# Two kernels in one: halves of k and v moved from the lower and upper partitions to the even and odd ones

## The chip, the cores and the metric

The kernel runs on one core of a Trainium2 chip. The metric is device time of one execution in microseconds: the median of three runs of the kernel before is 225.6 us, and they lie between 224.6 and 225.98. A profile of one further execution shows what each engine did. The engines are TensorE (PE; its weight loads are listed as PEld), VectorE (DVE), ScalarE (ACT), GpSimd (POOL) and SyncE (SP), which here only issues transfers.

## The reference

Two independent computations on 2048 tokens of 576 channels are placed side by side in the output.

```python
# A: attention of 32 heads (18 channels each) over 8 earlier tokens, two apart
q, k, v = split(x @ wqkv)
idx = pos[:, None] - 2 * arange(8)                 # masked where negative
a = softmax(einsum(q, k[idx]) * 18 ** -0.5) @ v[idx]
a = a.reshape(S, D) @ wo
# B: a short and a long causal convolution per channel, gated
k_shift = sum(k_pad[t : t + S] * shift_k[:, 3 - t] for t in range(4))
kv = k_shift * v
y = causal_convolution(kv, ssm_k) + kv * ssm_D     # length 2048, by FFT in the reference
b = q * y
out = concatenate([a, b], axis=-1)
```

## The kernel before

**Part A.** x is brought into transposed form (channels in partitions) in two ways. Its first two quarters of 512 tokens are loaded as they are (`load_x`, line 150) and turned on TensorE (`transpose_x`, `tail_x`, lines 403 to 412), then copied from PSUM by VectorE and ScalarE (lines 464 to 467 for the first quarter, 474 to 476 for the second). The second half comes by a transposing transfer (`turn_x`, line 207). Projections follow: `project_first` (line 433) for the first two quarters of q, then units of `project` (line 307). The logits are products on VectorE (line 647), summed over the channels of a head on TensorE (line 656); softmax runs on VectorE and ScalarE; the weights are spread over partitions by transfers on SP (line 724), multiplied with v on VectorE (line 746) and summed on TensorE (line 762); `output` (line 799) multiplies with wo.

**Part B.** The long convolution is done in four blocks of 512 tokens by matrix products with tables of sines. Each block is stored in two halves of 64 partitions. In the lower half, partition p holds seven consecutive rows of k, of which the last four are tokens 4p to 4p+3 of the block; the three before them serve the short convolution. The upper half holds the block's last 256 tokens mirrored, that is in descending order. `load_k` (line 157) and `load_v` (line 174) issue one transfer for each half; for the first block the low half is split, since rows before the first token don't exist: three rows of zeros (line 164), the first four tokens (line 165), and the rest in two pieces (line 168). `taps` (line 502) forms the short convolution on VectorE: four products and three sums per block, and a product with v (lines 507 to 511). Its coefficients `skb` must run forwards in one half and backwards in the other. The loop at line 445 makes them: a row of the coefficients is copied to all partitions by matmuls with a matrix of ones, `ones96`, one matmul for the lower 64 partitions and one for the upper 64. `mirror` (line 513) multiplies each block with the matrix `fold` (lines 228 to 231), which puts the sum of a token and its mirror image in one half and their difference in the other. The spectra of the filter (`filter_spectrum`, line 543, ps_fk) and of the blocks (`x_spectrum`, line 602, ps_fx), their products (line 883), sums (ps_z, line 903) and the inverse (ps_inv and ps_back, lines 935 to 976) follow; VectorE multiplies with q (line 989) and the result is stored.

**The order of the work.** The order of every engine is written out by the program. VectorE runs through tables, taps, logits, softmax, weighted sums and spectral products. TensorE's other work lies in a list of units, and at each step of VectorE's sequence the function `until` (line 283) issues as many units as the next number in the tuple `PLACES` (line 19) says. `need` issues units until those of a given name are done. SP's queue holds, in this order: x's first quarter in two transfers, the first third of the weights (`load_w(nc.sync, 0)`), x's second quarter, k's first block, the second third of the weights, `turn_x(0)`, v's first block, k's second block, `turn_x(1)`, v's second block, and later the rest. A transfer that reuses a semaphore waits for the one that used it before; there are eight. Before the first x arrives, `idle_work` (line 137) keeps TensorE busy with matmuls of zeros, four at the start and two after the coefficients.

**PSUM.** Two tags, A and B, of two buffers each, serve all results of TensorE; the coefficients use B, A and A in the three passes of the loop at line 445.

Of the kernel before, what the change touches and what calls it, by code (L numbers as in the profile page):

```python
# [12 lines left out]
ALU = mybir.AluOpType  # L13
FP32 = mybir.dt.float32
BF16 = mybir.dt.bfloat16
# [1 line left out]
PSUM = bass.MemoryType.PSUM  # L17

PLACES = (
    16, 6, 8, 11, 1, 0, 5, 2, 0, 4, 2, 4, 1, 0, 4, 2, 3, 0, 1, 2, 1, 3, 2, 4, 0, 1, 6, 3, 2, 6, 3, 5, 0, 7, 5,  # L20
    2, 4, 0, 0, 1, 2, 1, 0, 3, 0, 1, 0, 0, 0, 0, 5, 1, 0, 4, 0, 0, 3, 0, 0, 0, 3, 0, 4, 4, 1, 1,
)


def view(t, offset, dims):

    return bass.AP(tensor=t.tensor, offset=t.offset + offset, ap=[list(t.ap[0])] + [list(d) for d in dims])
# [3 lines left out]
def kernel(  # L31
# [13 lines left out]
    nc = tc.nc  # L45
    Bsz, S, D = A_x.shape
# [3 lines left out]
    xf = A_x.flatten_outer_dims()  # L50
    outf = out.flatten_outer_dims()
    qf = B_q.flatten_outer_dims()
    kf = B_k.flatten_outer_dims()
    vf = B_v.flatten_outer_dims()
# [14 lines left out]
    NBL, BL = 4, 512  # L69
# [18 lines left out]
    def bank2(name, tag):  # L88
        return pp.tile([128, 2, 512], FP32, name=name, tag=tag)
# [12 lines left out]
    def xT(kb, t0, n):  # L102
        return view(xw, XW + SPB * (t0 // 1024) + 1024 * kb + t0 % 1024, [[1, n]])

    def x5(jj):
        return view(xw, XW + SPB * jj + 4096, [[1, 512]])
# [14 lines left out]
    sp1 = s1.enter_context(tc.tile_pool(name="s1", bufs=1, reuse_waits="tile"))  # L121
# [6 lines left out]
    nc.scalar.dma_start(skrow[96:97, :], B_shift_k.rearrange("d j -> (d j)").unsqueeze(0))  # L128
    warm = sp1.tile([128, 1], FP32, name="warm")
    nc.scalar.activation(warm[:], pib[:], ACT.Sin)  # L130
    ones96 = sp1.tile([97, 64], BF16, name="ones96")
    nc.vector.memset(ones96[0:96, :], 0.0)
    nc.vector.memset(ones96[96:97, :], 1.0)
    nc.vector.memset(skrow[0:96, :], 0.0)
    ones0 = main.tile([128, 128], BF16, name="ones0")

    def idle_work(n):
        ps = bank2("ps_idle", "A")
        for _ in range(n):
            nc.tensor.matmul(ps[:, 0, :], zeros[:, 0:128], zeros, start=True, stop=True)  # L140
# [4 lines left out]
    xnat = view(Ks, 0, [[4 * D, 4], [D, 4], [1, D]])  # L145
# [1 line left out]
    kTok = main.tile([128, NBL, 4, D], BF16, name="kTok", tag="r_ktok")  # L147
    kjs, vts = [], []

    def load_x(qtr, sb0=0, n=4):  # L150
        r0 = 512 * qtr + 128 * sb0
        nc.sync.dma_start(xnat[:, qtr, sb0:sb0 + n], xf[r0:r0 + 128 * n, :].rearrange("(sb p) c -> p sb c", p=128))

    for sb in (0, 2):
        load_x(0, sb, 2)

    def load_k(i):

        eng = nc.sync
        kj = sp1.tile([128, 7, D], BF16, name="kj", bufs=2)  # L160
        r0 = BL * i
        low = [(0, 64)]
        if i == 0:
            nc.gpsimd.memset(kj[0:1, 0:3, :], 0.0)
            eng.dma_start(kj[0:1, 3:7, :], kf[0:4, :].unsqueeze(0))
            low = [(1, 49), (49, 64)]
        for p0, p1 in low:
            eng.dma_start(kj[p0:p1], bass.AP(tensor=kf.tensor, offset=kf.offset + (r0 + 4 * p0 - 3) * D,
                                             ap=[[4 * D, p1 - p0], [D, 7], [1, D]]))
        eng.dma_start(kj[64:128], bass.AP(tensor=kf.tensor, offset=kf.offset + (r0 + 256 + 3) * D,  # L170
                                          ap=[[4 * D, 64], [-D, 7], [1, D]]))
        kjs.append(kj)

    def load_v(i):
        vt = sp1.tile([128, 4, D], BF16, name="vt", bufs=2)
        nc.sync.dma_start(vt[0:64], vf[BL * i:BL * i + 256, :].rearrange("(p c) d -> p c d", c=4))
        nc.sync.dma_start(vt[64:128], bass.AP(tensor=vf.tensor, offset=vf.offset + (BL * i + 256 + 3) * D,
                                              ap=[[4 * D, 64], [-D, 4], [1, D]]))
        vts.append(vt)

# [13 lines left out]
    for gi, g in enumerate(GORD):  # L194
        sg = 1 - 2 * (g & 1)
        nc.gpsimd.iota(fr_i[:, gi, :], pattern=[[8 * sg, 128]], base=4096 * (g & 1) + sg * (2 * g + 1),
                       channel_multiplier=0)
    ones128 = sp1.tile([128, 128], BF16, name="ones128")
    nc.gpsimd.memset(ones128[:], 1.0)
    ident = main.tile([128, 128], BF16, name="ident")  # L200
    nc.gpsimd.affine_select(ident[:], ones128[:], pattern=[[1, 128]], compare_op=ALU.is_equal, fill=0.0,
                            base=0, channel_multiplier=-1)
# [4 lines left out]
    def turn_x(h):  # L207
# [15 lines left out]
    flip = main.tile([128, 128], BF16, name="flip")  # L223
    nc.gpsimd.affine_select(flip[:], ones128[:], pattern=[[1, 128]], compare_op=ALU.is_equal, fill=0.0,
                            base=-127, channel_multiplier=1)
    flipn = main.tile([128, 128], BF16, name="flipn")
    nc.gpsimd.tensor_scalar(flipn[:], flip[:], -1.0, None, op0=ALU.mult)
    fold = main.tile([128, 128], BF16, name="fold")
    for h in range(2):
        nc.gpsimd.tensor_copy(fold[0:64, 64 * h:64 * h + 64], ident[0:64, 0:64])  # L230
        nc.gpsimd.tensor_copy(fold[64:128, 64 * h:64 * h + 64], (flip, flipn)[h][64:128, 0:64])
    flip2 = main.tile([128, 128], BF16, name="flip2")
    nc.gpsimd.tensor_scalar(flip2[:], flip[:], 2.0, None, op0=ALU.mult)

# [1 line left out]
    for c0, p0, p1 in ((0, 0, 128), (128, 0, 128), (256, 0, 128), (384, 0, 128), (512, 0, 64), (512, 64, 128)):  # L236
        EHS.append(main.tile([128, 32], BF16, name=f"E{len(EHS)}"))
        e = EHS[-1][p0:p1, :]
        if p1 - p0 < 128:
            nc.gpsimd.memset(EHS[-1][64 - p0:128 - p0, :], 0.0)  # L240
        nc.gpsimd.affine_select(e, ones128[p0:p1, 0:32], pattern=[[-18, 32]], compare_op=ALU.is_ge, fill=0.0,
                                base=c0, channel_multiplier=1)
        nc.gpsimd.affine_select(e, e, pattern=[[18, 32]], compare_op=ALU.is_ge, fill=0.0,
                                base=17 - c0, channel_multiplier=-1)
# [3 lines left out]
                            fill=-1.0e9, base=-DIL * (W - 1), channel_multiplier=0)  # L248
# [125 lines left out]
    def table(n_i, T, vec, cols, period, offs):  # L374
        for n in range(2):
            nc.vector.tensor_scalar(n_i[:, n, :], vec, rp[:, cols[n]:cols[n] + 1], offs[n], op0=ALU.mult, op1=ALU.add)
        nc.vector.tensor_single_scalar(n_i, n_i, period - 1, ALU.bitwise_and)
        return lambda: nc.scalar.activation(T, n_i, ACT.Sin, bias=pib[:], scale=-2.0 * np.pi / period)

    def table_k(c):  # L380
        return table(n_all[:, 2 * c:2 * c + 2, :], TK[:, c, :, :], n_all[:, 8, :], (c, c), 2048, (512.0, 0.0))

    def table_x(n):
        n_i = view(qk, 4096 * n + 1024, [[2048, 2], [1, 1024]]).bitcast(I32)
        return table(n_i, TX[:, 2 * n:2 * n + 2, :], n_all[:, 8, :], (4 + 2 * n, 5 + 2 * n), 4096,
              (offx[:], offx[:]))
# [16 lines left out]
    def transpose_x(qtr, pts, kb0, sbs):  # L403
        for kb in (kb0, kb0 + 1):
            for sb in sbs:
                nc.tensor.transpose(pts[:, kb - kb0, 128 * sb:128 * sb + 128],
                                    xnat[:, qtr, sb, 128 * kb:128 * kb + 128], ident[:])

    def tail_x(qtr, pt):
        for sb in range(4):  # L410
            nc.tensor.transpose(pt[64 * qtr:64 * qtr + 64, 0, 512 + 128 * sb:640 + 128 * sb],
                                xnat[:, qtr, sb, 512:576], ident[:], tile_position=(0, 64 * qtr))

    def copy_tail(qtr, pt):
        r = slice(64 * qtr, 64 * qtr + 64)
        nc.scalar.activation(x5(0)[r], pt[r, 0, 512:1024], ACT.Copy)

    def pair_x():
        return pp.tile([128, 2, 1024], BF16, name="ps_x", tag="B")
# [13 lines left out]
    def project_first(jp, ct0):  # L433

        ps = bank2("ps_proj", "A")
        for e in range(2):
            c0 = 128 * (ct0 + e)
            for kb in range(4):
                nc.tensor.matmul(ps[:, e, :], wq(kb, 0, c0, 128), xT(kb, 512 * jp, 512), start=(kb == 0), stop=False)  # L439
        for e in range(2):  # L440
            nc.tensor.matmul(ps[:, e, :], wq(4, 0, 128 * (ct0 + e), 128)[64 * jp:64 * jp + 64],
                             x5(0)[64 * jp:64 * jp + 64], start=False, stop=True, tile_position=(64 * jp, 0))
        nc.scalar.activation(view(q, S * ct0 + 512 * jp, [[S, 2], [1, 512]]), ps[:], ACT.Copy)

    for n0 in (512, 0, 256):
        n = min(256, D - n0)
        ps = bank2("ps_sk", "A" if n == 256 else "B")
        for h in range(0, n, 128):
            w = min(128, n - h)
            sk = skrow[:, 4 * (n0 + h):4 * (n0 + h + w)].rearrange("p (d j) -> p d j", j=4)  # L450
            for r in range(2):
                nc.tensor.matmul(ps[64 * r:64 * r + 64, h // 128, 0:4 * w], ones96[:],
                                 sk if r else view(skrow, 4 * (n0 + h) + 3, [[4, w], [-1, 4]]),
                                 start=True, stop=True, tile_position=(0, 64 * r))
        nc.scalar.activation(skb[:, :, n0:n0 + n],
                             ps[:].rearrange("p b (d j) -> p j (b d)", j=4)[:, :, 0:n], ACT.Copy)
    sines = [table_k(0), table_k(1)]
    idle_work(2)
    pts = [pair_x() for _ in range(2)]
    for sbs in ((0, 1), (2, 3)):  # L460
        for n in range(2):
            transpose_x(0, pts[n], 2 * n, sbs)
    tail_x(0, pts[1])
    for n in range(2):
        nc.vector.tensor_copy(xT(n, 0, 512), pts[0][:, n, 0:512])
        nc.scalar.activation(xT(2 + n, 0, 512), pts[1][:, n, 0:512], ACT.Copy)
    copy_tail(0, pts[1])
    sines += [table_x(0), table_x(1), table_k(2), table_k(3)]
    project_first(0, 0)
    pts = [pair_x() for _ in range(2)]  # L470
# [98 lines left out]
    for i in range(NBL):  # L569
        r = taps(i)  # L570
# [450 lines left out]
    for n, (j, t, i) in enumerate(todo):  # L1021
# [3 lines left out]
        r = sums(j, t, i, *prs.pop(n))  # L1025
# [43 lines left out]
```

## Time and profile before

| | |
|---|---|
| median of three runs | 225.6 us (224.6 to 225.98) |
| the profiled execution | 225.71 us, of which span 224.0 |
| granted TensorE clock, mean | 0.987 of full speed |
| busy: TensorE, VectorE, ScalarE, GpSimd | 210.8, 208.0, 155.0, 34.3 us |
| transfers | 31.4 MB, 140 GB/s on average over the span |
| first product of the taps | 17.32 us after the span's start |
| first logits product | 62.87 us |

The span runs from the first to the last instruction that the profile has; the execution's own time holds a little more. Busy time is the time in which an engine works on at least one instruction. In a list in order of time, the first two numbers of a line are start and duration (for merged instructions the duration from the first to the last), the number behind the x is how many were merged, and the bracket says how long the engine was idle before and what it waited for. In the lists of waits the numbers are total microseconds, times, and the longest.

### The profile page before, as it was taken

How to read it: one execution, taken by the hardware profiler on the slowest of the kernel's cores; microseconds unless marked ns; L12 is line 12 of the kernel's file. 1: busy time of each engine (PE TensorE's matmuls, PEld its weight loads, DVE VectorE, ACT ScalarE, POOL GpSimd, SP SyncE). 2: the span in 40 equal slices, each digit the busy share in tenths (PEclk: the TensorE clock that was granted, in tenths of full speed). 3: DMA queues.
4: the chain of work that ended last, by engine and by line, in shares of the span. 5: the costliest groups of instructions: out<-in, count | busy, mean ns of one | idle time of the engine just before them, and what ended most of it. 6: DMA issues, size and time to landing. Idle time of an engine off the chain costs nothing.

```text
span 224.0 us, 5300 instructions
## 1 busy us (share of the span) xinstructions
PE 210.8 (94%) x2258; PEld 117.4 (52%) x2268; DVE 208.0 (93%) x154; ACT 155.0 (69%) x213; POOL 34.3 (15%) x71
## 2 busy tenths in 40 slices
PE   7869988999999999999999999999999999999892
PEld 2433343444575556663444446665656667667561
DVE  7958969999998999999989999999999899999992
ACT  5454799897676997655566758885678887655631
POOL 8981000000000040404320000005000000330000
PEclk9979999999999999999999999999999999999998
DMA  5999999999920038568999469907311103662016
GB/s 174 255 215 183 219 215 219 220 190 236 230 55 0 3 58 155 96 116 151 197 207 234 122 115 205 245 6 217 104 56 53 57 3 107 196 215 69 3 49 162
DMA packets 31001, 31.41 MB, mean 140 GB/s; under 512 B 16865, under 2 KB 26721, under 8 KB 30978
## 3 DMA queue, kind: packets, MB, share of 16 engines
q1 hardware_dynamic: 25728, 21.92, 45.5%
q0 software_dynamic: 2624, 6.64, 14.1%
q10 hardware_dynamic: 2626, 2.52, 3.3%
q8 instruction: 17, 0.28, 0.5%
q14 instruction: 6, 0.05, 0.1%
HBM read 13.11 MB, written 4.72 MB: 80 GB/s over the span
## 4 chain that ended last, share of the span: by engine, by line
PE 56%; DVE 15%; DMA 11%; ACT 7%; issue 4%; SPq 4%; DVEq 0%; ACTq 0%
PE ps_fk L538 9%; PE ps_wo L815 7%; PE ps_proj L311 6%; DVE qk L883 6%; PE ps_z L903 5%; DMA X<-attn 5%; PE ps_fk L539 5%; DMA Ks<-in_A_x_dram 4%; PE ps_inv L935 4%; PE ps_acc L762 3%; DVE P L746 3%; PE ps_log L656 3%; PE ps_proj L439 3%; SPq L724 3%; PE ps_fx L609 3%
## 5 line engine op out<-in xcount | busy, mean ns | idle before, releaser
L883 DVE TENSOR_TENSOR qk<-xw,Ks 128x3072 bf16<-128x3072 bf16 x30 | 50.5, 1753 | 1.2 <-PE ps_z L903 1.0
L647 DVE TENSOR_TENSOR prod<-qk 128x4096 bf16<-128x4096 bf16 (+1 forms) x20 | 40.6, 2075 | 2.7 <-PE ps_log L656 2.6
L311 PE MATMUL ps_proj<-xw 128*128 128x512 bf16 x151 | 36.9, 380 | 1.6 <-ACT qk L347 0.9
L538 PE MATMUL ps_fk<-kTok,TK 128*128 128x384 bf16 x128 | 32.8, 327 | 0.2 <-ACT Ks L553 0.2
L539 PE MATMUL ps_fk<-kTok,TK 128*128 128x192 bf16 x128 | 31.4, 246 | 0.0
L553 ACT ACTIVATE Ks<-ps_fk 128x576 bf16<-128x576 f32 x32 | 20.5, 655 | 9.6 <-PE ps_fk L539 9.4
L311 PEld LDWEIGHTS <-xw 128*128 128x128 bf16 x160 | 14.5, 98 | 19.9 <-issue 5.8
L916 ACT ACTIVATE Yall<-ps_z 128x768 bf16<-128x768 f32 x23 | 17.4, 808 | 6.1 <-PE ps_z L903 5.9
L612 ACT ACTIVATE xw<-ps_fx 128x576 bf16<-128x576 f32 x32 | 18.6, 661 | 0.2
L538 PEld LDWEIGHTS <-TK 128*128 128x128 bf16 x128 | 12.5, 98 | 11.8 <-issue 4.2
L815 PE MATMUL ps_wo<-qk,pv 128*128 128x288 bf16 x128 | 17.9, 287 | 0.0
L609 PE MATMUL ps_fx<-ab,TX 64*128 64x288 bf16 x256 | 17.7, 283 | 0.0
L347 ACT ACTIVATE qk<-ps_proj 128x1024 bf16<-128x1024 f32 x14 | 14.4, 1030 | 3.8 <-PE ps_proj L323 2.0
L510 DVE TENSOR_TENSOR ab<-ab,tB 128x2304 bf16<-128x2304 bf16 x12 | 16.3, 1358 | 0.4
L903 PE MATMUL ps_z<-qk,ident 64*64 64x384 bf16 x288 | 16.4, 325 | 0.3 <-ACT pv L766 0.3
L507 DVE TENSOR_TENSOR tB<-kj,skb 128x2304 bf16<-128x2304 bf16 x12 | 16.3, 1356 | 0.3
L935 PE MATMUL ps_inv<-Yall,TI 128*128 128x288 bf16 (+1 forms) x112 | 15.5, 292 | 0.7 <-ACT Yall L916 0.6
L762 PE MATMUL ps_acc<-P,ident 64*64 64x512 bf16 x192 | 15.3, 379 | 0.0
L347 ACT ACTIVATE v<-ps_proj 128x1024 bf16<-128x1024 f32 x9 | 9.2, 1022 | 8.8 <-PE ps_proj L323 4.7
L609 PEld LDWEIGHTS <-TX 64*128 64x128 bf16 x256 | 11.7, 94 | 6.5 <-issue 3.6
L872 POOL DMA_DIRECT2D qB<-in_B_q_dram x4 | 2.9, 732 | 78.8 <-DMA out_dram<-qB 41.6
L822 ACT ACTIVATE qk<-ps_wo 128x576 bf16<-128x576 f32 x16 | 10.4, 651 | 6.1 <-PE ps_wo L815 3.2
(154 smaller groups left out, 361.7 us busy)
## 6 DMA issues: line engine op xcount, KB each, us to landing
kj<-in_B_k_dram SPq DMA_DIRECT2D x7, 504.0 KB, 7.9
Ks<-Ks POOLq DMA_DIRECT2D x6, 576.0 KB, 7.7
qk<-attn SPq DMA_DIRECT2D x12, 256.0 KB, 5.4
vt<-in_B_v_dram SPq DMA_DIRECT2D x8, 288.0 KB, 8.5
out_dram<-qk ACTq DMA_DIRECT2D x8, 288.0 KB, 3.3
X<-attn SPq DMA_DIRECT2D x8, 256.0 KB, 5.6
xw<-in_A_wqkv_dram SPq DMA_DIRECT2D x2, 576.0 KB, 8.4
qB<-in_B_q_dram POOLq DMA_DIRECT2D x4, 288.0 KB, 3.9
```

The costliest lines, as they stand in the source:

```text
L311: nc.tensor.matmul(ps[:, jp, :], wq(kb, comp, 128 * ct, 128), xT(kb, 1024 * jj + 512 * jp, 512), start=(kb == 0 and not first), stop=(kb = ...
L347: nc.scalar.activation(view(t, o + pad + 1024 * jj, [[512, 2], [1, 512]]), ps[:], ACT.Copy)
L538: nc.tensor.matmul(o[:, 0:2], w, rhs[:, 0:2], start=start, stop=stop)
L539: nc.tensor.matmul(o[:, 2], w, rhs[:, 2], start=start, stop=stop)
L553: nc.scalar.activation(view(Ks, (3 - m) * SPB + 4 * D * cs + 96 * gi, [[768, 3], [384, 2], [1, 96]]), acc3(ps), ACT.Copy, scale=(CSG, SSG) ...
L609: nc.tensor.matmul(ps[:, pm, 0:HD], TX[64 * pm:64 * pm + 64, c, 128 * gi:128 * gi + 128], kv[64 * pm:64 * pm + 64, c, HD * h:HD * h + HD], ...
L647: r = dve(1024 * nj, lambda: nc.vector.tensor_tensor(view(prod, 0, [[256 * nj, 4], [256, nj], [1, 256]]), view(t, o + 256 * hh, [[0, 4], [ ...
L762: nc.tensor.matmul(acc[64 * o:64 * o + 64, h, :], ident[64 * h:64 * h + 64, 64 * h:64 * h + 64], view(P, 256 * u, [[2048, 2], [1, 256]])[6 ...
L815: nc.tensor.matmul(ps[:, r, 0:HD], oT(hh, j + 2 * r, t)[:, o:o + 128], wo[:, t // 2, t % 2, HD * h:HD * h + HD], start=(t == 0 and h == 0) ...
L883: r = dve(3072, lambda: nc.vector.tensor_tensor(pr, view(xw, i * SPB + 4 * TH * t, [[4 * D, 2], [0, 2], [1, 4 * TH]]), view(Ks, (3 - j + i ...
L903: nc.tensor.matmul(view(acc[r], 512 * h, [[192, 2], [96, 2], [1, 96]])[o:o + 64], w[64 * h:64 * h + 64, 64 * h:64 * h + 64], pr[64 * h:64 ...
L935: nc.tensor.matmul(ps[:, c, 0:n], TI[:, sl, pm, 128 * c:128 * c + 128], Yall[:, j % 2, pm, sl, c0:c0 + n], start=(pm == 0 and sl == 0), st ...
```

## The change

The two halves of each block of k and v change places: the first half goes to the even partitions 0, 2, ..., 126 and the mirrored half to the odd ones 1, 3, ..., 127. What follows from this: `fold` is now made by two selections for each of its halves (ones where p = 2m, and plus or minus one where p = 127 - 2m); `ones96` becomes two matrices of 128 columns, one with ones in the even columns and one in the odd, and each pair of coefficient matmuls now writes all 128 partitions and is accumulated. Besides, x's first quarter is loaded by one transfer instead of two; the first four tokens of k are loaded from POOL's queue instead of SP's; the two matmuls of zeros after the coefficients go; the coefficients are made in two steps before x's first quarter is turned and one step after it; the first quarter is turned in one go over its four row blocks instead of two times two; and some numbers of PLACES differ. Line numbers behind line 133 shift by one to four.

```diff
 PLACES = (
-    16, 6, 8, 11, 1, 0, 5, 2, 0, 4, 2, 4, 1, 0, 4, 2, 3, 0, 1, 2, 1, 3, 2, 4, 0, 1, 6, 3, 2, 6, 3, 5, 0, 7, 5,
-    2, 4, 0, 0, 1, 2, 1, 0, 3, 0, 1, 0, 0, 0, 0, 5, 1, 0, 4, 0, 0, 3, 0, 0, 0, 3, 0, 4, 4, 1, 1,
+    16, 6, 8, 11, 1, 0, 5, 1, 1, 3, 3, 4, 1, 0, 3, 3, 4, 0, 1, 2, 1, 3, 2, 4, 0, 1, 6, 1, 0, 9, 3, 5, 1, 7, 5,
+    2, 4, 0, 0, 1, 1, 2, 0, 3, 0, 1, 0, 0, 0, 0, 5, 0, 1, 4, 0, 0, 3, 0, 0, 0, 4, 0, 3, 3, 1, 1,
 )
...
-    ones96 = sp1.tile([97, 64], BF16, name="ones96")
-    nc.vector.memset(ones96[0:96, :], 0.0)
-    nc.vector.memset(ones96[96:97, :], 1.0)
+    ones96 = sp1.tile([97, 256], BF16, name="ones96")
+    nc.vector.memset(ones96[:], 0.0)
+    nc.vector.memset(ones96[96:97, 0:128:2], 1.0)
+    nc.vector.memset(ones96[96:97, 129:256:2], 1.0)
...
-    for sb in (0, 2):
-        load_x(0, sb, 2)
+    load_x(0)
...
-            eng.dma_start(kj[0:1, 3:7, :], kf[0:4, :].unsqueeze(0))
+            nc.gpsimd.dma_start(kj[0:1, 3:7, :], kf[0:4, :].unsqueeze(0))
             low = [(1, 49), (49, 64)]
         for p0, p1 in low:
-            eng.dma_start(kj[p0:p1], bass.AP(tensor=kf.tensor, offset=kf.offset + (r0 + 4 * p0 - 3) * D,
+            eng.dma_start(kj[2 * p0:2 * p1:2], bass.AP(tensor=kf.tensor, offset=kf.offset + (r0 + 4 * p0 - 3) * D,
                                              ap=[[4 * D, p1 - p0], [D, 7], [1, D]]))
-        eng.dma_start(kj[64:128], bass.AP(tensor=kf.tensor, offset=kf.offset + (r0 + 256 + 3) * D,
+        eng.dma_start(kj[1:128:2], bass.AP(tensor=kf.tensor, offset=kf.offset + (r0 + 256 + 3) * D,
                                           ap=[[4 * D, 64], [-D, 7], [1, D]]))
...
-        nc.sync.dma_start(vt[0:64], vf[BL * i:BL * i + 256, :].rearrange("(p c) d -> p c d", c=4))
-        nc.sync.dma_start(vt[64:128], bass.AP(tensor=vf.tensor, offset=vf.offset + (BL * i + 256 + 3) * D,
+        nc.sync.dma_start(vt[0:128:2], vf[BL * i:BL * i + 256, :].rearrange("(p c) d -> p c d", c=4))
+        nc.sync.dma_start(vt[1:128:2], bass.AP(tensor=vf.tensor, offset=vf.offset + (BL * i + 256 + 3) * D,
                                               ap=[[4 * D, 64], [-D, 4], [1, D]]))
...
     for h in range(2):
-        nc.gpsimd.tensor_copy(fold[0:64, 64 * h:64 * h + 64], ident[0:64, 0:64])
-        nc.gpsimd.tensor_copy(fold[64:128, 64 * h:64 * h + 64], (flip, flipn)[h][64:128, 0:64])
+        f = fold[:, 64 * h:64 * h + 64]
+        nc.gpsimd.affine_select(f, ones128[:, 0:64], pattern=[[-2, 64]], compare_op=ALU.is_equal, fill=0.0,
+                                base=0, channel_multiplier=1)
+        nc.gpsimd.affine_select(f, f, pattern=[[2, 64]], compare_op=ALU.not_equal, fill=(1.0, -1.0)[h],
+                                base=-127, channel_multiplier=1)
...
-    for n0 in (512, 0, 256):
+    def spread_taps(n0):
         n = min(256, D - n0)
         ps = bank2("ps_sk", "A" if n == 256 else "B")
...
-                nc.tensor.matmul(ps[64 * r:64 * r + 64, h // 128, 0:4 * w], ones96[:],
+                nc.tensor.matmul(ps[:, h // 128, 0:4 * w], ones96[:, 128 * r:128 * r + 128],
                                  sk if r else view(skrow, 4 * (n0 + h) + 3, [[4, w], [-1, 4]]),
-                                 start=True, stop=True, tile_position=(0, 64 * r))
+                                 start=(r == 0), stop=(r == 1))
...
+    spread_taps(512)
+    spread_taps(0)
     sines = [table_k(0), table_k(1)]
-    idle_work(2)
     pts = [pair_x() for _ in range(2)]
-    for sbs in ((0, 1), (2, 3)):
-        for n in range(2):
-            transpose_x(0, pts[n], 2 * n, sbs)
+    for n in range(2):
+        transpose_x(0, pts[n], 2 * n, range(4))
...
     copy_tail(0, pts[1])
+    spread_taps(256)
     sines += [table_x(0), table_x(1), table_k(2), table_k(3)]
     project_first(0, 0)
```

More of the change, by code (lines that the diff above doesn't have):

```diff
@@ L148, with load_x @@
     kjs, vts = [], []
-    def load_x(qtr, sb0=0, n=4):
-        r0 = 512 * qtr + 128 * sb0
-        nc.sync.dma_start(xnat[:, qtr, sb0:sb0 + n], xf[r0:r0 + 128 * n, :].rearrange("(sb p) c -> p sb c", p=128))
-    for sb in (0, 2):
-        load_x(0, sb, 2)
+    def load_x(qtr):
+        nc.sync.dma_start(xnat[:, qtr], xf[512 * qtr:512 * qtr + 512, :].rearrange("(sb p) c -> p sb c", p=128))
+    load_x(0)
     def load_k(i):
```

## The prediction

> **What bounds the kernel now.** I read the page first (busy shares), then who waits for whom on VectorE and TensorE, then the opening in order of time, then busy time and transfer rate in stretches, last the DMA view of the opening. The profiled execution took 225.71 us (span 224.0, so 1.7 lie around it); the median of the runs shown is 225.6, so I count from 225.7.
>
> ```profile
> PE 210.8 (94%) x2258; PEld 117.4 (52%) x2268; DVE 208.0 (93%) x154; ACT 155.0 (69%) x213; POOL 34.3 (15%) x71
> ```
> Two engines are nearly full, so a gain on one alone is stopped by the other. Who waits:
>
> ```profile
> DVE ab L507 <- DMA kj<-in_B_k_dram: 4.4, 2, 2.7
> DVE prod L647 <- PE ps_log L656: 2.6, 6, 0.6
> ...
> PE ps_x L406 <- DMA Ks<-in_A_x_dram: 1.9, 1, 1.9
> ```
> VectorE's largest idle time is for k, twice; after that it waits 2.6 us for TensorE in the logits and little else. TensorE's longest wait is for x's second quarter. In order of time:
>
> ```profile
> 12.73 1.16 PE L406 MATMUL ps_x<-ident,Ks 128*128 128x128 bf16 x16 [1.88 <-DMA Ks<-in_A_x_dram]
> ...
> 14.79 2.77 PE L439 MATMUL ps_proj<-xw 128*128 128x512 bf16 x7 [0.33 <-issue]
> ...
> 17.32 1.36 DVE L507 TENSOR_TENSOR ab<-kj,skb 128x2304 bf16<-128x2304 bf16 x1 [2.73 <-DMA kj<-in_B_k_dram]
> ...
> 18.02 1.90 PE L439 MATMUL ps_proj<-xw 128*128 128x512 bf16 x8
> ...
> 29.97 1.36 DVE L507 TENSOR_TENSOR ab<-kj,skb 128x2304 bf16<-128x2304 bf16 x1 [1.68 <-DMA kj<-in_B_k_dram]
> ```
> Seven projection matmuls took 2.77 us at 14.79, eight took 1.90 at 18.02: the first stood under a half clock. The stretches show when (columns: PE, PEld, DVE, ACT, POOL busy, granted clock, DMA share, GB/s):
>
> ```profile
> 6.00:9.00 3.00, 2.63 (x25) 1.67 (x24) 2.97 (x8) 1.39 (x4) 2.79 (x7) 1.00 1.11 329
> 9.00:12.00 3.00, 1.85 (x8) 0.49 (x6) 2.93 (x7) 1.52 (x3) 2.79 (x7) 1.00 0.99 149
> 12.00:15.00 3.00, 1.94 (x21) 1.57 (x23) 2.52 (x5) 0.51 (x1) 2.58 (x9) 0.76 1.07 209
> 15.00:18.00 3.00, 3.00 (x9) 0.85 (x7) 0.68 (x1) 2.02 (x3) 2.31 (x8) 0.67 1.41 236
> ```
> If the clock is either 1 or 0.5, 0.76 and 0.67 make 0.48 x 3 + 0.66 x 3 = 3.4 us at half clock, from about 13.6 to 17.0, right behind the gap in which TensorE waited for x. The last column holds the other fact: 329 GB/s while x and the weights (128 partitions each) move, 149 while the 64-partition halves of k do, at the same DMA share. The engines are as busy and carry half. In the trace's packet records, 8064-byte packets of k's low half that start between 8.1 and 8.6 us take 0.34 to 0.41 us; between 9.5 and 10.7 us, when all engines send to the same 64 partitions, 0.77 to 0.96. The last 1152-byte packets of x's second quarter fall into that crowd (0.12 to 0.18 us each against about 0.06 before), which is why it lands 9.1 us after its issue.
>
> **The change, part by part.**
>
> *Halves in even and odd partitions.* Each k and v transfer still writes 64 partitions and as many bytes, but across the whole range. Its rate is not in this trace: one end is today's 149 GB/s (no gain), the other the 329 of the 128-partition transfers. I take about 300, because rate follows the partitions reached in the rows above. [...]
>
> k's first block: by 9 us the stretches have carried 3 x (81 + 274 + 329) = 2.05 MB. x's two quarters and the first weights are 1872 KB, the block's halves 1008 KB, together 2.95 MB; the missing 0.9 MB take 3.0 us at 300 GB/s or 4.3 at 209, so until 12.0 to 13.3, and up to 1.5 us for the slowest engine: landed by 13.5 to 14.8 instead of 17.3. VectorE ends its tables at 14.59. The first wait (2.73) shrinks to 0 to 0.2. Second block: its issue on SP stands at 20.45, behind the transposing x load, which waits for x's second quarter (12.70) and holds SP 5.97 us. With x landing about 1.5 us earlier and the transfer about 3 us shorter it lands near 25.5 to 26; VectorE comes for it at 14.7 + 11.2 = 25.9. The second wait (1.68) shrinks to 0 to 0.5. **VectorE: 3.9 to 4.4 us earlier**; ends 0 and 4.4.
>
> *x's second quarter.* If k's packets no longer crowd the same partitions, x's last packets keep their early pace and it lands at 10.5 to 11.5, not 12.69. TensorE ends its first projection at 10.85, so at most 1.88 us are to be had. **I take 1.5**; ends 0 and 1.88.
>
> *The half clock.* With that gap nearly closed, TensorE is busy from 10.2 to 13.6 and the 3.4 us at half clock should not follow: at most 1.7 us, less what stood still anyway (0.33). **I take 1.4**; ends 0 and 1.7.
>
> *x's first quarter in one transfer.* One issue of 0.59 us (row of the second quarter) for two of together 0.97; weights and second quarter are issued 0.38 us earlier. The transposes now need all of it. The halves landed 3.2 us after issue, so by about 5.1; the taps' matmuls hold TensorE until 5.2. Cost 0. The other end is 9.1 us, the landing of the second quarter: the slow rival below.
>
> *k's first row on POOL.* Saves SP 0.41 us. POOL comes to it after its memset (4.05), issues for 0.72 (Drow's row) and lands 4.8 us later: 9.6, before 14.6. With the 11.8 of wo's issues it would be 16.6, and 2.0 of the 2.73 us come back. Behind it POOL's queue is 0.72 later: fold is first used at 39.7, the E matrices at 67.1, Drow near 97, so cover is ample. Four selects for four copies (1.68 us) cost the same within 0.5, under the same cover.
>
> *Taps.* Ten 64-column matmuls ran in 2.13 us because the two column halves overlap. Now six of 128 columns stand before the transposes (about 2.2 at the early spacing of 0.42) and four behind them (4 x 0.23 = 0.9, or 1.7 at half clock). The two idle matmuls (1.01) go. The four fall between transposes that now end near 7.2 and the first projection, which waits for weights and VectorE's copies until 8.25. Cost 0 at full clock; 0.7 if not, out of the slack before x. ACT's third copy (1.02) moves behind x's copies, into ACT's 1.39 us wait at 10.89. VectorE's two more small memsets, 0.2 us, lie ahead of tables that end before k lands.
>
> *PLACES.* Same matmuls, some fillers moved: eight logit matmuls ahead of one filter unit, 16 ps_fx matmuls (1.07 us) from before the first ps_acc to behind it. That product ends at 120.84 and TensorE would now come at 121.04, so nothing is lost.
>
> **Sum.** TensorE is 1.5 + 1.4 = 2.9 us earlier from 17 us on. The copies and sines that fill ACT from 25.0 to 36.6 start from TensorE's projections and move along. VectorE is 4.2 ahead, but from 63 to 100 us TensorE is busy 37.0 of 37 us: VectorE's lead turns into waits for the logits. TensorE has 2.3 us idle between 100 and 216, little of it usable. So the smaller shift decides: 225.7 - 2.9 = **222.8 us**; on its own 221.5 (VectorE's lead wins) to 223.8.
>
> **Rivals.**
> 1. *The half clock stays* (27%): the wait shrinks, but the clock still halves for one such stretch; gain 1.5, 224.2. For it: the granted clock fell after about 2 idle us, the transposes are short, and two idle matmuls are dropped from 5.5 to 6.5. If the clock then opens only at 10.2, taps and first projection end near 12.3 and the gain falls to 0.4: 225.3. Against it: the projection now runs straight into the transposes. [...]
> 2. *Spreading does nothing* (9%): k's rate is bound by its packets or by two transfers at once, the change doesn't do what it says; 0.38 us from the issues: 225.3. Against it: 0.4 against 0.8 us for the same packet.
> 3. *Slower: x's first quarter lands late* (12%). In one piece it may take 9.1 us like the second quarter and land at 9.9 instead of 5.1. TensorE then stands still from 5.3 to 9.9, and behind such a gap I count half clock up to 13.6: 2.2 us of transposes, 1.7 of taps, then at full clock 2.6 of projection and 1.7 for the second quarter's transposes, which end at 18.1 instead of 14.45. Of these 3.6 us late 1.2 come back, since the half clock no longer lies on 14.5 to 17.0: 2.4 lost, 228.1. It decides once the landing is later than about 7.6 (7.6 + 1.6 + 0.9 + 2.65 = 12.7, when the second quarter comes today). Against it: nothing is ahead of it in the queue, and the halves took 3.2.
>
> **Numbers.** Forecast 52%, rivals 27, 9 and 12. A change under 1% (2.26 us) can't be told from none. Below 223.3: most of the forecast's share and the case where TensorE's later idle time is used too, 51%; within, 37%; slower, 12%. The range 221.5 to 226.0 leaves out the slow rival.
>
> **What would show it.** Rate in 9 to 12 us near 300 GB/s; first transposes of the second quarter near 11; granted clock 1.00 from 12 to 18; first taps product at 14.6 to 15, the second block's with no wait; VectorE's waits on ps_log above 2.6 us. I am wrong if k still lands after 17, if the clock drops again, or if VectorE's lead survives to the end.

## The result and the profile after

The changed kernel took 222.88 us, median of four runs (221.82 to 223.53), beside 225.47 for the kernel before (224.60 to 225.98): a ratio of 0.988 with a 95% interval of 0.983 to 0.993. In a later comparison it took 222.30 (221.82 to 222.89), ratio 0.984 (0.981 to 0.987). The forecast was 222.8. Its profiled execution took 223.0 us, of which the span is 220.9, so 2.7 less than before in time and 3.1 in span.

Busy time by engine:

```profile
PE 210.3 (95%) x2256; PEld 118.2 (53%) x2266; DVE 207.8 (94%) x155; ACT 154.8 (70%) x213; POOL 37.4 (17%) x72
```
The work is the same; it has moved closer together. The list of waits (total, times, longest):

```profile
DVE prod L651 <- PE ps_log L660: 3.2, 6, 1.0
...
DVE P L750 <- DMA X<-attn: 0.8, 1, 0.8
PEld L408 <- DMA Ks<-in_A_x_dram: 0.6, 1, 0.6
```
VectorE's 4.4 us of waiting for k are gone altogether, and so are TensorE's 1.88 for x's second quarter (the 0.6 left are for the first). In their place VectorE waits 0.6 us more for the logits, and 0.8 for a transfer that it did not wait for before: X, the softmax weights spread over partitions. In order of time (start, duration, engine, work, idle time before):

```profile
10.33 1.07 PE L408 MATMUL ps_x<-ident,Ks 128*128 128x128 bf16 x16
...
11.67 1.90 PE L441 MATMUL ps_proj<-xw 128*128 128x512 bf16 x7
...
14.48 1.36 DVE L511 TENSOR_TENSOR ab<-kj,skb 128x2304 bf16<-128x2304 bf16 x1
...
25.40 1.35 DVE L511 TENSOR_TENSOR ab<-kj,skb 128x2304 bf16<-128x2304 bf16 x1
...
63.73 2.29 DVE L651 TENSOR_TENSOR prod<-qk 128x4096 bf16<-128x4096 bf16 x1 [0.95 <-PE ps_log L660]
...
110.55 2.29 DVE L750 TENSOR_TENSOR P<-X,v 128x4096 bf16<-128x4096 bf16 x1 [0.84 <-DMA X<-attn]
```
The second quarter's transposes start at 10.33 instead of 12.73, without a gap. Both blocks' first taps products (14.48 and 25.40) start without a wait. The last two lines are where part of that lead is given back. The stretches of the opening (columns as before: five engines' busy time, granted clock, DMA share, GB/s):

```profile
6.00:9.00 3.00, 3.00 (x23) 1.55 (x21) 2.97 (x7) 2.31 (x5) 2.77 (x8) 1.00 1.15 302
9.00:12.00 3.00, 3.00 (x27) 1.66 (x27) 2.93 (x7) 1.75 (x3) 2.80 (x6) 1.00 0.99 228
12.00:15.00 3.00, 2.95 (x14) 1.10 (x13) 2.93 (x6) 2.95 (x4) 2.70 (x8) 1.00 1.32 301
15.00:18.00 3.00, 3.00 (x15) 1.02 (x13) 2.97 (x3) 1.40 (x2) 2.81 (x4) 1.00 1.00 224
```
The half clock of 12 to 18 us is gone (1.00 for 0.76 and 0.67). The rate between 9 and 12 us rose from 149 to 228 GB/s.

### The profile page after: what moved, and what is told of

It is laid out like the page before. It is cut to its first block, busy times and chain, and to the rows that moved or that the text cites. A ratio compares the mean times of both kernels' runs of the same rounds, so it can differ in the third digit from the quotient of the medians.

```text
span 220.9 us, 5301 instructions
## 1 busy us (share of the span) xinstructions
PE 210.3 (95%) x2256; PEld 118.2 (53%) x2266; DVE 207.8 (94%) x155; ACT 154.8 (70%) x213; POOL 37.4 (17%) x72
## 4 chain that ended last, share of the span: by engine, by line
PE 69%; DVE 11%; ACT 8%; DMA 5%; issue 4%; SPq 1%; DVEq 0%; ACTq 0%
PE ps_fk L542 10%; PE ps_proj L313 9%; PE ps_acc L766 7%; PE ps_wo L819 7%; DVE qk L887 6%; PE ps_z L907 5%; PE ps_fx L613 5%; DMA X<-attn 5%; PE ps_fk L543 5%; PE ps_inv L939 4%; PE ps_proj L441 3%; PE ps_log L660 3%; ACT qk L349 2%; DVE P L750 2%; PE ps_fold L523 2%
## 5 line engine op out<-in xcount | busy, mean ns | idle before, releaser
L750 DVE TENSOR_TENSOR P<-X,v 128x4096 bf16<-128x4096 bf16 x6 | 13.6, 2288 | 1.3 <-DMA X<-attn 0.8
```

## The experiments

All times of kernels below are medians; the kernel before took 225.52 us beside experiments 1 to 4, 225.68 beside 5 to 8, and 225.79 beside the repeats in 8 and experiment 9. What is read from a trace is that of one profiled execution of each kernel.

**1. The halves back in lower and upper partitions,** all else as changed.

```diff
-            eng.dma_start(kj[2 * p0:2 * p1:2], ...
+            eng.dma_start(kj[p0:p1], ...
-        eng.dma_start(kj[1:128:2], ...
+        eng.dma_start(kj[64:128], ...
```
(and v, `fold` and the ones to match)

> The changed kernel with the halves of k and v back in the lower and upper 64 partitions (fold and the ones matrix to match); everything else of the change stays: x's first quarter in one transfer, k's first row on POOL, order of the coefficients, no idle matmuls in the middle, new PLACES. Theory (spreading the halves over the partitions frees the transfers, and all else follows from that): about 150 GB/s from 9 to 12 us, x's second quarter lands after 11.5, k's first taps product starts after 16.5, TensorE idles over 1 us before the second quarter's transposes and a half-clock stretch returns; 225.3 us (224.6 to 226.0). Rival (the earlier issues on SP and the new order do it): first taps product before 15, 222.5 to 223.5 us.

Measured: 223.92 us (223.44 to 225.46), ratio 0.991 (0.988 to 0.995). The opening on TensorE and VectorE, and the stretch from 9 to 12 us:

```profile
10.68 1.07 PE L405 MATMUL ps_x<-ident,Ks 128*128 128x128 bf16 x16
...
28.00 1.36 DVE L508 TENSOR_TENSOR ab<-kj,skb 128x2304 bf16<-128x2304 bf16 x1 [1.69 <-DMA kj<-in_B_k_dram]
```

```profile
9.00:12.00 3.00, 3.00 (x28) 1.62 (x26) 2.93 (x7) 2.04 (x3) 2.84 (x6) 1.00 0.93 159
```
The rate is back at 159 GB/s, and yet x's second quarter landed 6.3 us after its issue (9.1 before, 6.4 in the changed kernel), TensorE has no gap and the clock stays at 1.00. So the spreading is not needed for x and the clock; something else in the change is enough. What the spreading alone still brings here is on VectorE: without it the second block's product waits 1.69 us for its k, and the first block's starts at 15.23 instead of 14.48, after 0.62 us of waiting. The time lies between the two that were expected (225.3 and 222.5 to 223.5): the theory that all follows from the spreading fails, and the rival (earlier issues and the new order) gives too short a time.

**2. The spreading alone,** on the kernel before: halves in even and odd partitions with their matrices, nothing else.

```diff
-            eng.dma_start(kj[p0:p1], ...
+            eng.dma_start(kj[2 * p0:2 * p1:2], ...
```

> The kernel before with only the halves moved to even and odd partitions (fold, the ones matrix and the accumulated coefficient matmuls to match); x's first quarter in two transfers, k's first row on SP, order, idle matmuls and PLACES as before. Theory: first taps product at 14.5 to 15, clock 1.00 from 12 to 18 us, 223.2 us (222.6 to 223.9). Rival (the issues on SP do it): first taps product after 16.5, 225 us or more. Rival (the new PLACES are needed to use the lead): opening as early as in the changed kernel, but 224.2 us or more.

Measured: 223.18 us (222.56 to 224.72), ratio 0.990 (0.982 to 0.998). x's second quarter landed 7.5 us after its issue, at 11.1:

```profile
11.17 1.07 PE L410 MATMUL ps_x<-ident,Ks 128*128 128x128 bf16 x16 [0.25 <-DMA Ks<-in_A_x_dram]
```
Neither block's product waited for k, and the clock was 1.00 from 12 to 18 us. This is just what the prediction had put down to the spreading. Both experiments hold together: either edit by itself closes most of TensorE's gap.

**3. The old table of places,** all else as changed.

```diff
-    16, 6, 8, 11, 1, 0, 5, 1, 1, 3, 3, 4, 1, 0, 3, 3, 4, ...
+    16, 6, 8, 11, 1, 0, 5, 2, 0, 4, 2, 4, 1, 0, 4, 2, 3, ...
```

> The changed kernel with the numbers of PLACES from before. Theory: 222.7 to 223.4 us, VectorE's waits on ps_log within 0.5 us of the changed kernel's 3.2. Rival (PLACES carry the gain): 224.2 us or more, with TensorE waiting for ps_acc or VectorE for ps_log.

Measured: 222.52 us (221.85 to 223.44), ratio 0.985 (0.979 to 0.991); waits for the logits 3.2 us as in the changed kernel. The places carry none of the gain.

**4. TensorE's gap filled with zeros,** on the kernel before: the clock is kept up, and k and x come as they did.

```diff
     project_first(0, 0)
+    idle_work(9)
```

> The kernel before with nine more matmuls of zeros behind the first projection, so that TensorE has no gap before x's second quarter comes; k and x land as before. It tells what an earlier TensorE alone is worth. Expected of the clock: 1.00 from 12 to 18 us, TensorE's next projections 1.2 to 1.5 us earlier. Theory (the smaller shift decides, and VectorE's is zero): 225.0 to 225.6 us. Rival (TensorE's shift alone sets the end): 223.9 to 224.4 us.

Measured: 225.84 us (224.94 to 228.47), ratio 1.001 (0.998 to 1.005). The clock in the stretches and VectorE's first taps product:

```profile
12.00:15.00 3.00, 3.00 (x30) 1.90 (x28) 2.88 (x6) 0.76 (x1) 2.69 (x7) 1.00 1.07 208
15.00:18.00 3.00, 3.00 (x14) 1.09 (x15) 0.66 (x1) 2.93 (x4) 2.21 (x8) 1.00 1.61 197
```

```profile
17.34 1.36 DVE L508 TENSOR_TENSOR ab<-kj,skb 128x2304 bf16<-128x2304 bf16 x1 [2.39 <-DMA kj<-in_B_k_dram]
```
The half clock is gone with the gap, and TensorE begins its list of projections 0.74 us earlier (22.02 for 22.76), not the 1.2 to 1.5 that were expected. VectorE's first logits product stands at 62.87, where it stood before, and the time gets no shorter. A TensorE that is earlier alone, by this much, gained nothing.

**5. x's first quarter in one transfer, alone,** on the kernel before.

```diff
-    for sb in (0, 2):
-        load_x(0, sb, 2)
+    load_x(0)
```

> The kernel before with one edit: x's first quarter in one transfer instead of two; halves of k and v, k's first row, taps and order stay. Theory A (the two transfers delay x's second quarter): it lands by 10 us, TensorE has no gap before the second quarter's transposes, the granted clock is 1.00 from 12 to 18, the first taps product starts at 15 to 16.5 and the second block's waits about 1.7 us for its k; the end goes by VectorE, at 223.9 us (223.3 to 224.6). Rival B (k's first row on SP, or the crowd of k's halves, delays it): a gap of over 0.5 us stays and the time is 225 or more.

Measured: 224.24 us (223.68 to 225.75), ratio 0.994 (0.990 to 0.998).

```profile
11.12 1.07 PE L404 MATMUL ps_x<-ident,Ks 128*128 128x128 bf16 x16
...
14.89 1.36 DVE L505 TENSOR_TENSOR ab<-kj,skb 128x2304 bf16<-128x2304 bf16 x1
...
27.73 1.36 DVE L505 TENSOR_TENSOR ab<-kj,skb 128x2304 bf16<-128x2304 bf16 x1 [1.76 <-DMA kj<-in_B_k_dram]
```
This one line lets x's second quarter land 6.2 us after an issue that is 0.46 earlier (9.3 instead of 12.7), takes away TensorE's gap and half clock, and even the first block's wait for k; only the second block still waits. Theory A held. What goes with it in the packet records stands in the section on the hardware.

**6. The same edit undone** in the changed kernel.

```diff
-    load_x(0)
+    for sb in (0, 2):
+        load_x(0, sb, 2)
```

> The changed kernel with x's first quarter in two transfers again, all else as changed. Theory A (two transfers delay x's second quarter, spreading k helps it a little): x's second quarter lands at about 11 us, its transposes start at about 11.2, single 1152-byte packets of x take over 0.4 us between 4 and 7 us, the clock stays at 1.00; 223.2 us (222.6 to 223.8). Rival B (the order of issues on SP alone): lands by 10 us, 222.9.

Measured: 223.48 us (222.95 to 223.91), ratio 0.989 (0.983 to 0.996). x's second quarter landed 7.8 us after its issue, at 11.4; TensorE waited 0.79 us for it, and the clock stayed at 1.00. Theory A again. Some waiting for k comes back too: 0.44 us before the second block's product. Since k's first row is on POOL in this kernel, and on SP in that of experiment 5, that step is not what moves x.

**7. x's second quarter behind k's first block** in the changed kernel: VectorE keeps its lead, TensorE gets its gap back.

```diff
     load_w(nc.sync, 0)
-    load_x(1)
...
     load_k(0)
+    load_x(1)
```

> The changed kernel with x's second quarter issued behind k's first block. Theory A (the smaller of the two shifts decides): x's second quarter lands at 13 to 14 us, TensorE stands 2.5 to 3.5 us before its transposes, some 3.4 us at half clock follow, VectorE's first taps product still starts at 14.5 or earlier, and the lead of VectorE turns into waits for the logits: 225.5 to 226.5 us. Rival B (VectorE's lead sets the end): about 223.

Measured: 226.40 us (224.42 to 228.26), ratio 1.002 (0.998 to 1.006).

```profile
12.85 1.89 PE L408 MATMUL ps_x<-ident,Ks 128*128 128x128 bf16 x16 [2.45 <-DMA Ks<-in_A_x_dram]
...
14.48 1.36 DVE L511 TENSOR_TENSOR ab<-kj,skb 128x2304 bf16<-128x2304 bf16 x1
```

```profile
12.00:15.00 3.00, 2.15 (x20) 1.96 (x20) 2.93 (x6) 0.00 (x0) 2.70 (x8) 0.62 1.22 288
15.00:18.00 3.00, 3.00 (x13) 0.98 (x11) 2.96 (x3) 2.53 (x3) 2.81 (x4) 0.81 1.03 246
```

```profile
DVE prod L651 <- PE ps_log L660: 7.2, 6, 4.9
```
Behind a gap of 2.45 us the half clock is back (0.38 x 3 + 0.19 x 3 = 1.71, or 3.4 us at one half). VectorE starts its taps at 14.48 and its first logits product at 58.30, 4.57 us ahead of the kernel before, and then stands 7.2 us instead of 2.6 waiting for the logits: 4.6 more, the whole of its lead. Rival B is out.

**8. The filter's last turn behind wo's loads** in the changed kernel. A turn is two transfers of 576 KB from POOL's queue that add one part of the filter's spectrum to another; there are three, and the one moved here, `turn_filter(1)`, is the last (the expectations call it the second). Its transfers then no longer start among X's.

```diff
-            if (gi, cs) == (3, 1) and m < NBL - 1:
+            if (gi, cs) == (3, 1) and 0 < m < NBL - 1:
...
+    turn_filter(1)
     nst = [0]
```

> The changed kernel with the second turn of the filter issued behind wo's loads instead of among the matmuls before X's spread. Theory A (the turn's transfers delay X's): X lands within 7.5 us of its issue instead of 11.6, VectorE does not wait for it at its first weighted product (0.84 us in the changed kernel), and the time is 222.1 us (221.6 to 222.5). Rival B (the wait only moves, to TensorE or to the filter's own transfer): no gain, 222.9.

Measured: 222.23 us (221.82 to 222.45), ratio 0.984 (0.977 to 0.990); no wait for X. To see whether that is more than a difference between comparisons, it ran again, beside the changed kernel and beside itself with the old places:

> The changed kernel itself once more, beside the kernels with the late turn on one chip: 222.9 us if its 222.88 holds; 222.3 or below if the difference to the late turn was that of two chips.

> The changed kernel with the second turn of the filter behind wo's loads, once more: if X's wait of 0.84 us is what it saves, 222.2 us and 0.5 to 0.8 below the changed kernel of the same call; if not, within 0.3 of it.

> The changed kernel with the second turn of the filter behind wo's loads and the old table of places. Theory A (the places carry nothing): no wait for X, the same as with the late turn alone, 222.2 us. Rival B (the 0.36 us that the old places showed beside the changed kernel is real and adds to the late turn): 221.9 us or below.

Measured: the changed kernel 222.30 us (221.82 to 222.89), with the late turn 221.83 (221.80 to 222.35), with the late turn and the old places 222.02 (221.83 to 222.15). The DMA view gives X's last transfer (KB, us from issue to landing), first in the changed kernel, then with the late turn:

```profile
X<-attn SPq DMA_DIRECT2D x1, 256.0 KB, 11.6
```

```profile
X<-attn SPq DMA_DIRECT2D x1, 256.0 KB, 6.2
```
And VectorE's product that needs it, with the late turn:

```profile
109.62 2.28 DVE L750 TENSOR_TENSOR P<-X,v 128x4096 bf16<-128x4096 bf16 x1
```
The mechanism is shown: with the turn's transfers beside it X's takes 5.4 us longer, and without them the wait is gone. What it is worth in time is 0.47 us by these medians, less than the 0.65 of the first comparison, and the runs overlap; a kernel better than the changed one by so little is likely but not proven. The old places add nothing.

**9. x's first quarter in two transfers of another cut,** even and odd partitions.

```diff
-    load_x(0)
+    for par in range(2):
+        nc.sync.dma_start(xnat[par:128:2, 0], bass.AP(tensor=xf.tensor, offset=xf.offset + par * D,
+                                                     ap=[[2 * D, 64], [128 * D, 4], [1, D]]))
```

> The changed kernel with x's first quarter in two transfers of another cut: even partitions in one, odd in the other, each with all four 128-row blocks. Theory A (two transfers of that quarter hold up what follows, however it is cut): single 1152-byte packets take over 0.4 us between 4 and 7 us, x's second quarter lands 7.5 to 8 us after its issue, at 11.0 to 11.6; 223.4 us (222.9 to 224). Rival B (only the cut by row blocks does): no such packets, 6.2 to 6.6 us after its issue, at about 10; 222.9.

Measured: 226.24 us (224.90 to 227.99), ratio 1.002 (0.999 to 1.006), which neither theory gave. The time has another cause, in the list of waits:

```profile
POOL Ks L197 <- DMA Ks<-in_A_x_dram: 3.8, 1, 3.8
...
DVE Ks L380 <- POOL Ks L197: 2.8, 1, 2.8
```
With x's rows written to every other partition, POOL's tables of numbers, which lie in another part of the same buffer, wait for x, and VectorE's sines for them: a new wait that the edit brought with it. The packets still answer the question: eight took over 0.4 us, as theory A says. x's second quarter landed 7.2 us after its issue, between the two forecasts and nearer theory A's 7.5.

## Why the prediction was right, and where its steps were not

**The smaller shift decides: shown, to a tenth of a microsecond.** Three places in the trace say how much earlier than before each engine is: TensorE at the start of its list of projections, VectorE at its first logits product, and VectorE's first weighted product. In the kernel before:

```profile
22.76 1.90 PE L311 MATMUL ps_proj<-xw 128*128 128x512 bf16 x8
...
62.87 4.49 DVE L647 TENSOR_TENSOR prod<-qk 128x4096 bf16<-128x4096 bf16 x2
...
113.69 2.29 DVE L746 TENSOR_TENSOR P<-X,v 128x4096 bf16<-128x4096 bf16 x1
```
And in the changed kernel, whose weighted product at 110.55 stands in the profile after:

```profile
18.77 1.90 PE L313 MATMUL ps_proj<-xw 128*128 128x512 bf16 x8
...
58.29 4.49 DVE L651 TENSOR_TENSOR prod<-qk 128x4096 bf16<-128x4096 bf16 x2
```
If the smaller of the first two shifts decides, and the wait for X is taken off, the third follows (all in us):

| kernel | TensorE earlier | VectorE earlier | wait for X | smaller less wait | measured |
|---|---|---|---|---|---|
| gap filled (4) | 0.74 | 0.00 | 0 | 0.00 | -0.06 |
| x in one, alone (5) | 3.20 | 2.23 | 0.65 | 1.58 | 1.58 |
| halves back (1) | 3.64 | 1.96 | 0 | 1.96 | 2.06 |
| spreading alone (2) | 3.15 | 4.28 | 0.23 | 2.92 | 2.90 |
| x in two (6) | 2.92 | 3.70 | 0.62 | 2.30 | 2.27 |
| x behind k (7) | -0.01 | 4.57 | 0.33 | -0.34 | -0.33 |
| changed kernel | 3.99 | 4.58 | 0.84 | 3.15 | 3.14 |
| late turn, again (8) | 3.99 | 4.58 | 0 | 3.99 | 4.07 |

The five traces that the table leaves out (experiments 3 and 9, the changed kernel again, the first late turn, and that with the old places) fit to 0.09 us. VectorE's last instruction is earlier by the same as its first weighted product to within 0.25 us, except in experiments 3 and 5, which gain 0.6 more on the way. The medians scatter more: those of the table's kernels moved by up to 0.6 us less than its last column says, and the changed kernel's by 2.59 and 3.49 in its two comparisons.

Experiment 4 moves TensorE alone and 7 VectorE alone, and neither gains. VectorE's lead did turn into waits for the logits, as predicted (2.6 to 3.2 us, the 0.6 that it is ahead of TensorE; 7.2 in experiment 7). That the forecast's number came out so closely is in part luck, through two misses that offset each other: TensorE's shift was 3.99 instead of 2.9, and 0.84 of it went into a wait that the prediction did not have.

**VectorE's 3.9 to 4.4 us** measured 4.58. Both waits for k went, and the second block's product starts at 25.40, where 25.5 to 26 was forecast. Two statements of this step were off. The rate between 9 and 12 us was to be near 300 GB/s and was 228; 300 is reached before and behind it. And the first block's wait does not need the spreading: with x in one transfer alone it was gone as well (experiment 5). The spreading is what takes the second block's wait away (1.76 and 1.69 us without it, in experiments 5 and 1): k's transfers of 504 KB for that block took 5.0 to 6.7 us in the ten kernels with the halves spread, and 7.4 to 8.0 in the four without. The packets show the same: k's packets of 8064 bytes took 0.60 to 0.61 us in the median with the halves in lower and upper partitions, in four kernels, and 0.31 to 0.39 in the ten with them in even and odd ones. Why, no run here shows.

**x's second quarter: the step that failed.** It was to land at 10.5 to 11.5 because k's packets no longer crowd the same partitions. It landed at 9.5, and not for that reason: without the spreading it landed just as early (experiment 1). As a statement on the spreading alone the step was good (11.1 in experiment 2). What it missed is in the next step, *x's first quarter in one transfer*, priced at nothing but 0.38 us of earlier issues. That edit alone brings x's second quarter from 12.7 to 9.3, and 1.4 us of time. The prediction had looked at the crowded packets from 9.5 us on and not at the slow ones between 4 and 7.

**TensorE's 3.99 us,** from one profiled execution to the other, come apart so: the gap 1.88 (predicted 1.5), the half clock 1.59 (predicted 1.4; from the transposes' start to the list of projections it is 10.03 us before and 8.44 after), and 0.52 because the first projection ended that much earlier (10.33 for 10.85), which the prediction had not counted. The taps' new place cost nothing, as it said.

**The half clock** followed its gap in every profiled execution: it is there behind gaps of 1.88 us (before) and 2.45 (experiment 7), and absent behind 0.25 and 0.79 (experiments 2 and 6) and none. In the kernel before, the clock fell at about 13.6 us, 0.8 us into the transposes, and reads 0.50 from 14.0 to 16.5 us. In experiment 7, 0.38 x 3 us at a half make 2.28 us before 15, so it fell at about 12.7, ahead of the first transpose at 12.85 and 2.3 us after the last matmul, which ended at 10.40.

The prediction took its 1.4 us from one profiled execution, and most executions do not have that half clock. Each execution's mean granted clock is on record. A stretch of 3.41 us at a half in a span of 224 us makes it 0.992 at most. Of the 49 executions of the kernel before that the comparisons use, 41 have 0.994 or more, with a median span of 223.4 us; eight have 0.986 to 0.989, with 225.0. So the half clock of the profiled one (clock 0.987, span 224.0) is not part of what the medians lost, and TensorE was probably earlier in most executions already, which no trace here shows; by experiment 4, that brings nothing while VectorE waits for k. In experiment 7, where VectorE is early, it does cost: of the nine executions that its comparison uses, the four of 0.994 or more have spans of 222.7 to 223.1 us, the five others 224.4 to 225.3. All nine executions of the changed kernel have 0.994 or more, so rival 1 is out for this change.

**Rival 2** (spreading does nothing) is out by experiment 2, and **rival 3** (x's first quarter lands late) by its landing 4.2 us after issue; it can't decide before 7.6 us and was there at about 5.

**The cover that gave way.** X's spreading was not in the prediction. Before, X's last transfer was issued at about 102.7 us and took 10.9, so it landed at about 113.6; VectorE came for it at 113.69. That cover was some 0.1 us. In the changed kernel VectorE comes 4.0 earlier; X is issued 4 us earlier too, but the transfer takes 0.7 longer, 11.6, and the cover is gone. The last turn's transfers run beside it in both kernels (issued at 101.19 to 103.6 us before, at 97.18 to 99.6 after). A step that is reached earlier needs its transfers earlier and as fast, and the prediction asked this for k and x only.

**The rest.** k's first row on POOL was to land at 9.6 us and came at 11.3, 7.3 us after its issue at 4.00 and not 4.8; the first taps product at 14.48 hides it. The four selects took 1.0 us for the copies' 1.7. PLACES cost and gave nothing (experiments 3 and 8). k's row on POOL alone, the taps' order alone and the two matmuls of zeros alone were not tried; all of them together with PLACES are the difference between experiment 2 (223.18) and experiment 6 (223.48), so no gain of theirs can be seen.

## What to carry to other kernels

When two engines are both nearly full, work out each one's shift by itself and count on the smaller; then ask of every transfer that the earlier work will need next how much cover it has, because the lead is first spent there. An edit priced at nothing because it "only" changes how a load is issued deserves a look at the packets behind it: here it moved another load by 3 us. Before a step is priced from one profiled execution, the granted clocks of the others say whether it happens in them too. And parts of a change can be substitutes: spreading alone gave 2.3 us, one transfer alone 1.4, both together 2.6 to 3.5.

## What the runs showed of the hardware that was not expected

**Two transfers in place of one, and slow packets behind them.** In the five kernels that load x's first quarter in two transfers (before, and experiments 2, 4, 6 and 9), 5 to 9 packets of 1152 bytes took over 0.4 us, the longest 0.87 to 1.15, in the 3.6 us from about 3.8 us on; the median packet there took 0.05. In all nine kernels with one transfer there is none in that time, and the longest took 0.11 to 0.23. Before it, in the first 2 us of such packets, all fourteen kernels have two to seven that took over 0.4 us. In the 3.6 us 0.95 to 1.07 MB of such packets went out with two transfers, and 1.21 to 1.26 with one (0.84 where k's first block is issued ahead). It is not the cut by row blocks: even and odd partitions do it too. Why two transfers of half the size, issued 0.5 to 0.8 us apart, hold single packets up is not explained by any run here.

**One load's issue reached three others.** With x in one transfer alone (experiment 5), k's first block is issued 0.45 us earlier, its first packet starts 5.65 us after the first of all 1152-byte packets instead of 6.18, and the block is there by 14.89 us instead of 17.32, with its halves where they were before. That fewer packets are held up ahead of it is a likely reason, not a shown one.
